# A new written-out order for a two-layer attention and token-MLP kernel: the same operations, other places and other engines

## The chip, the cores and the metric

The kernel runs on one core of a Trainium2 chip. Its time is device microseconds of one execution. Five engines work beside each other, each through its own list of instructions: TensorE (PE in the profile, its weight loads PEld), VectorE (DVE), ScalarE (ACT), GpSimd (POOL) and SyncE (SP), which here only issues DMAs. An instruction that needs the result of another engine waits for a semaphore, and everything behind it on its engine waits too.

## The reference

A stream x of 2048 rows and 512 columns (bf16) passes through four residual steps, A, B, A, B, with the same weights in both rounds. This text calls one round of A and B a layer (layer 1 and layer 2; the code counts 0 and 1).

```
A: h = layernorm(x); q, k, v = h @ wqkv, 32 heads of 16
   p = softmax(q k^T / 4), each row sees itself and the 255 rows before it
   x = x + (p v) @ wo
B: h = layernorm(layernorm(x)); u = gelu(h^T @ w1 + b1), w1: 2048 x 1792, over the rows
   x = x + (u @ w2 + b2)^T, w2: 1792 x 2048
```

## The kernel before, in words

x stays in SBUF as 16 tiles of 128 rows. The rows are taken in four blocks of 512 (the m of `qkv`); in layer 1 the first block is split in two halves of 256. For each tile, `ln_blocks` takes statistics on DVE (L471, L473), the reciprocal deviation as a power on POOL (L484), and the normalised tile xh on DVE (L491). xh is transposed, the first tiles on PE with an eviction by ACT or DVE (L549, L556, L558), all later ones by DMA (L542). Q, K and V are projected by matmuls (L513, which is the line of all matmuls made by the helper `mm_group`).

K is stored "block diagonal" (`kbd`), the two head halves beside each other with zeros between. It gets there straight from PSUM (L582 on ACT, L583 on DVE), or through a staging tile (L594, L596) and then in one of three ways: two masked copies on POOL or DVE (L609) or eight DMAs (L604). V goes into a staging tile (L631 on DVE, L633 on ACT), and four DMAs make the V blocks `vb` (L636).

Attention runs in chunks of 256 or 512 rows. A step of a chunk is a score group on PE (L690, 4 heads at a time), two exponentials on ACT (L705, `pt<-PS`), one to three masks on POOL or DVE (L726), and the weighted sums on PE (L747, operation `pv`). The sums are transposed on DVE (L767), divided (L771, L773 on POOL or DVE) and transposed back (L778). `wo_block` multiplies by wo and adds to x (L789).

B's first product is cut in parts over the rows (`PARTS`): parts whose rows are ready run between the score groups as filler for PE (`u_part`), the last part (L868, `u_last`) runs after the attention, then the gelu on ACT (L883) and the product with w2 (L513, `y_block`), whose result DVE adds to x (L909). In layer 1 these last products run on into the beginning of layer 2's attention; in layer 2 each result tile is stored at once (L955), and the last tile in three pieces (`y_last`, L895, L898).

Weights w1 and w2 come in loads of 128 KB (L803, L815), x, wqkv and wo in loads of 128 to 512 KB (L401, L405, L416). All of SP's loads go through one queue.

The order is written out. The operations are recorded with what they read and write, some of them with alternatives (another engine for the same result: `alts`, for the evictions, masks, products, K copies). `begin_order` decodes `ORDER`, a packed list that names, position by position, the next operation and which alternative it takes; `replay` walks it, hands out buffers in that order and appends each operation to its engine's list; `emit` writes the lists with the waits that the reads, writes and buffer reuse need. No cost or due time is looked at when the kernel is built.

```
        for pos, (idx, alt) in enumerate(order):
            o = self.ops[idx]
            o.eng, o.fn = o.alts[alt][:2]
            self._take(o)
            self.order[o.eng].append(o)
```

Of the kernel before, what the change touches and what calls it, by code (L numbers as in the profile page):

```python
# [11 lines left out]
P = 128  # L12


ORDER = (
    'c-qBQJ&5a87Cw^iym#m24ro9DE$D$>P@zHr1r$&~4;*kn0Tl{p!G#}q!G!|~IH1A-2lN&PwBQ9TIN-tyE*x;-!V50EV3sLdcwrV?xbVUhQ@EI7Sf+5{!o?nq'
    '$20ciz5Hx8yJyB%_g-CH-SeIAd`ALMAW$=FmRTW@UM>_MC=^Pi;EO_mPE}Ps8;@00Q*G-bFh2xcf8YPD^Jy4{4r?wJVNeNZF(i;5j)u<AALc&kTb8BtuoYXD'
    'EV9&YSZ!4!>!g`bN{ewkFV?-!CZqniE{d#Ft%9xV!b#)(TCEaPYV5=_a)q2Md&JD;Y}-<ZEX(4%qNtz|nGh-nqM(nNFd2`>41lrbFj=oV>y08w5=@sO5l;Q9'
    'E5~t`4k7c4g`?**4MwApcs`k)PYEH@>2%p2_m%ug%J;zU^<}w}Bmj_HTwbUu%%gUDrPRKHF)ZpZ8V-j>IkgT#q9zGxwOWL+*Q6H5QAD5FVugcBIS8UCVtAx5'
    'oJ<&u19$iv7cna1#_*YKJ5^OyJ|z~OtkC_q)3F@aao}aY-|XcJja+V-4ePd#=6Nr5$8=54^GwtKgfnf&d1+c%n=zA#x^CzI129br?M|l+Elo!hRD}YZf_Qqu'  # L20
    'SP)3ERD?p|W-T+p<AlWmmz&J>+$%~ixu#_`=S`xiFBAY-2B_6)1cnJql2x_3URO7ptD9B5K6*wd)Vkd{-aVgQFQ<Q>cFUdVVsW`#OsA3K%;)o&*{hi55Q9-J'
    '&$FfBG&||^{?_aDDLp%bAP7veKNy<kcP63}C9PHz{n0aH$ElgsxDhjE)LBq-b-g0Gt{ca(`sEk$b^TQ&DrE65;-xkz7100?E&w~1%|a*V<m_xVrnDCQ9!bX-'
    'm1YXX*h}M)fU!Om&@okIOl(PvC5<{j12J|S3bq}Tigu~!`;_{gMNNZdeg7q;j;bwzsGwS!B?u~0Ziq%Y!^?{V8oI8Zce{fD0`^>Em^H0dLzbj46plFn<Ww=A'
    'FQK`4LOj>DNP1RH&t|jQXq06s1sG+39kbi*t^uyE!Cc~!i-kgzrhK_Xo{tGG>%nMzHqPfML1rY`Bx!fr#C02P^EJAFZ(cjutY58xXXjs)hPF-A3lBL3pX4lJ'
    'o4RQ@9~cBgQ$#}$1OcwgE@B2$AdHBjArra3DN3SFkg5WD1k-axgz>l%2E(u)1b&%$CBINMT;FsZMb~r1oPiq~IYiJfbj!AeLw#WAgbe9`w0dBuuGqvgRI6$j'
    'Lc4<2z`#YeO+!o3Fn0_>IzT9qQcL7U7do+6@7L?yx^*Vrn%pXe80Su@MFqwhm|>=H;=0V37#a(!ArlQI2rlNJAe`WqOfhG#%;{=H-5W~sx^x5=7q*a+gflh$'
    'eZw$Pt#TZr6a%Qw`y4VQmouyne9JOS0EC7qvVzDPj44PKNl{G8B<pp1eIlAyme0J)%S%H$)eL|an)+N(`aLv4B*F~_HO#v|s2W6@$RDsi$nbjkB_tw<aCUYk'
    '2%!wcfUen!F_|78BN06ngymAB$TM;-Nt5|()|t)vvzaWn&qvv;Tm`7MhvtWaKA@`N30<K-=(ly9A_Jd|R8$)In<f)_y+1(=bS0n$TwlMwx<cq7j=u@(C`omM'
    's+WpyhcVx0`At5b6!LM*{CvrmDw0$xmkNc#rysW*%d#2dEs#FcKqmsA;wpwx&^1K`SfV3>fB;P<6ID1nqf~>FlQsVIBw?qUO$1{_QR7&{n2;j^pNrDz@KvRP'
    'TuK<mIr4oZ1y_!9SyUwYJ76btI<*!T3yU5b?QZw{9Hy=d9K2`0HxPs}^t#>t;Lp8&uVtQFrU}$Q`lqt{ZNl~Yf`ICa&~-Y75XsujO{=A87$B%rB7GV}b(9zY'  # L30
    '!{`(WoNg6MMP0AzkT0PA69N(@pXYm16Wzfq^z*(fYqEw}a{7X?cLkw<Ig%y~Rv3X&ok}t$2N6%!f^;N~$NkaC$qf0x1Uyf>-6bt(Dr%$g90?}?KF5_9Bjq&r'
    '9VRfOm7H#+>+RW`V$C>FkB<j`i7}q|K(_<XYPW`Ah;7)b*Etl+sQ&d=xDeCKb@TZ=swXnG*RcqAC>3m#2FEZ|10}nJyGwXDa!fJMLOcUE@4D;t8rCTF_KdDp'
    '|1^yA<<&pVaphmfWICUu<!>~UB*XY_G#-s?$tqjlN}AScVXSKL*K!D9S_VJ=yjH4~LRu`AgEE#cl(BpvpVe)WwLK4sNQCSM`bXp=iwJ^1G+BAkm!89|;E<#0'
    '5m!-^W`k?os-6+90>f~bsiaDi{tQqkm1!RJ6VNdN6KJ;<Xrpm^*cw#FsDIU@*6DORRU@vZyI^4JQ7JM?MU+}7R=i5t^UGK(hjfISwCi<9P;1@T^KGmPwx6?$'
    '*`}Si72oo#we1*=ty>Z<K|oE*NRs|kQo3VFj-qBWDr2RP%}Py=YhYMbK*X6DDpU<N!bV@P(lwST5xh&(i+Q7GS|c{pKw4GeK!HfSMw)Ln+D&j%-rOMigkF)W'
    'tIbAOU&8!+J`XM&6!y_r8jXS!q*_hOK?T1v(t@EBna)rd<f<%4h$aS4NQ;jOl%l*~OW_w9_o&0&&v3hj+gnZ!duhI<*Czn)Jlx^9hb0`)bV%+FN`XV$Zku+n'
    '%>ZN|?LN&sO}kq=zHOhv-X((zp6<=U-J8*Pa_H5QU5DrIHq7vcHy#^*d!K)d4tMK5e>l${9Ua~EIN<K_y7Py7!t>njX^wjX)W6uc-L~877SOvn4xM=XCjR#3'
    'ffxM4i0An?kYc;%9Wwk|$-{APJ07>ksr#_L-FWzK8n-+D0aDygj{&!b@9tr^=Pk!^+<%y7KZ6b2k1gcj|6*(}X#Cwjf54*cklzn(I)3MF&FvFM_fPP5OiFd)'
    'PDWB$dFT6#-?q>0yM*KRNS1zT!}g1NyGbT<D<hdyr!twhb1?I;1+K~*&h7>o9{)0XkL(?vf4BgDKjPoOZ+@F@{L_OaPq}pBkzPEK;jMa+EjG7q-XVq8Cxq-~'
    'fqY-CA5M)9kj(yDwjO2Pn4mw1SmuWW<UnaM{7ypdNwS?t+e|9Z`@ub6^$)5i|0od;xd4x4`DbU#p|J1k!A{$`U5U8saSyKSuRIv-&+SBsdzd5tlMLqG#I842'  # L40
    'njg9Q>mP6%x*dvl<9p-|jZg3K-1a{$!)bv|s~^WdEIxed;iHG!)%)G|$*<zszX32A5e)'
)

def begin_order(n):
# [944 lines left out]
```

## Time and profile before

| | |
|---|---|
| median of 3 runs (lowest to highest) | 437.09 us (436.16 to 437.51) |
| the profiled execution, its own time | 436.27 us |
| its span | 434.5 us |
| granted TensorE clock | 1.0 |
| PE busy | 420.9 us, 97% of the span |
| DVE busy | 322.6 us, 74% |
| ACT busy | 317.0 us, 73% |
| POOL busy | 187.2 us, 43% |
| chain that ended last, by engine | PE 73%, ACT 18%, DVE 6%, DMA 1%, POOL 1% |
| 304 exponentials on ACT | 281.0 us, 1036 ns each |
| 189 masks on POOL, 77 on DVE | 125.9 us, 686 ns each; 29.6 us, 404 ns each |

A line of a group of instructions gives source line, engine, operation, tile written <- tiles read, count, busy us and mean ns. The chain follows the last instruction back to what released it, step by step. A mean over the whole span hides that the stages have different limits, so the table by stretches of time below says more than the shares above.

### The profile page before, as it was taken

Reading aid. Unit: us, or ns where it says so; the run is one execution under the profiler, and the core shown is the slowest. Engines: PE = TensorE matmul, PEld = TensorE weight load, DVE = VectorE, ACT = ScalarE, POOL = GpSimd, SP = SyncE. Lnnn points to the kernel's source line nnn. Section 1 sums busy time; section 2 is a strip of 40 time slices with the busy share of each in tenths; the row PEclk is TensorE's granted clock in tenths of the full one; section 3 lists DMA queues with packets and bytes.
Section 4 is the critical chain, followed back from the end, with each engine's and each line's share of the span. In section 5 each row is a group of like instructions: output and inputs, shape, how many; then the busy total and the mean of one; then the engine's idle time right before and its main releaser. Section 6 shows DMA issues by size and latency. Waiting matters only on the chain.

```text
span 434.5 us, 14318 instructions
## 1 busy us (share of the span) xinstructions
PE 420.9 (97%) x6177; PEld 188.5 (43%) x6177; DVE 322.6 (74%) x629; ACT 317.0 (73%) x364; POOL 187.2 (43%) x277
## 2 busy tenths in 40 slices
PE   7979989999999999999999999999999999999997
PEld 6534333434444444444444444444434444445443
DVE  7998989779996678556777999989788758422205
ACT  5999999999997953606999999899999870520000
POOL 7788865864664620011465554365435221000000
PEclk9999999999999999999999999999999999999999
DMA  8565262302163257723542282240223262747713
GB/s 237 167 125 88 63 127 37 79 5 49 26 166 83 75 152 211 208 62 88 137 110 52 64 147 64 51 77 11 47 64 99 66 175 69 226 140 213 228 32 115
DMA packets 101850, 46.03 MB, mean 106 GB/s; under 512 B 32156, under 2 KB 101788, under 8 KB 101788
## 3 DMA queue, kind: packets, MB, share of 16 engines
q1 hardware_dynamic: 101788, 45.13, 41.7%
q8 instruction: 49, 0.80, 0.8%
q14 instruction: 13, 0.11, 0.1%
HBM read 33.56 MB, written 2.10 MB: 82 GB/s over the span
## 4 chain that ended last, share of the span: by engine, by line
PE 73%; ACT 18%; DVE 6%; DMA 1%; POOL 1%; issue 0%; SPq 0%
PE PS L513 50%; ACT pt L705 17%; PE PS L868 8%; PE PS L690 8%; PE PS L747 7%; DVE stats L471 1%; DMA vb<-vst 1%; DVE xh_sb L491 1%; DVE pt L726 1%; DVE rl L767 1%; DMA x_sb<-in_A_x_dram 1%; POOL pt L726 0%; DVE stg L594 0%; DVE vst L631 0%; SPq L636 0%
## 5 line engine op out<-in xcount | busy, mean ns | idle before, releaser
L705 ACT ACTIVATE pt<-PS 128x1024 bf16<-128x1024 f32 (+1 forms) x304 | 281.0, 1036 | 13.1 <-PE PS L690 11.9
L726 POOL TENSOR_TENSOR pt<-pt,ldm 128x256 int32<-128x256 int32 (+2 forms) x189 | 125.9, 686 | 101.7 <-ACT pt L705 101.1
L513 PE MATMUL PS<-xhT,wqkv 128*128 128x512 bf16 (+1 forms) x288 | 67.8, 357 | 2.7 <-ACT pt L705 1.9
L513 PE MATMUL PS<-xh_sb,w1b 128*128 128x512 bf16 x280 | 69.9, 381 | 0.1
L513 PE MATMUL PS<-uT,w2b 128*128 128x512 bf16 (+2 forms) x308 | 68.3, 360 | 0.0
L690 PE MATMUL PS<-qT,kbd 32*128 32x64 bf16 (+4 forms) x1552 | 60.2, 247 | 3.1 <-ACT pt L705 2.1
L484 POOL TENSOR_TENSOR rstd<-agg,mhalf 128x2 f32<-128x2 f32 (+1 forms) x33 | 23.8, 722 | 66.8 <-DVE agg L473 66.7
L909 DVE SCALAR_TENSOR_TENSOR x_sb<-PS,bcol,x_sb 128x512 bf16<-128x512 f32 x31 | 22.6, 746 | 38.0 <-PE PS L513 37.7
L690 PEld LDWEIGHTS PS<-qT,kbd 32*128 32x128 bf16 x1552 | 22.7, 92 | 61.7 <-ACT pt L705 45.6
L767 DVE STREAM_TRANSPOSE rl<-PS 128x1024 f32<-128x1024 f32 x32 | 39.9, 1248 | 12.3 <-PE PS L747 12.1
L747 PE MATMUL PS<-pt,vb 64*17 64x128 bf16 (+4 forms) x3104 | 43.6, 248 | 2.4 <-DMA vb<-vst 1.1
L471 DVE BATCH_NORM_STATS2 stats<-x_sb 128x6 f32<-128x512 bf16 x64 | 44.2, 693 | 1.5 <-DMA x_sb<-in_A_x_dram 0.8
L883 ACT ACTIVATE uT<-rl,bcol 128x512 bf16<-128x512 f32 x28 | 18.3, 712 | 33.8 <-DVE rl L879 33.8
L513 PEld LDWEIGHTS PS<-uT,w2b 128*128 128x128 bf16 x308 | 27.5, 98 | 31.1 <-issue 3.2
L747 PEld LDWEIGHTS PS<-pt,vb 64*17 64x17 bf16 x3104 | 31.8, 84 | 17.6 <-issue 7.9
L513 PE MATMUL PS<-uT,pt 128*128 128x512 bf16 x168 | 39.2, 379 | 0.0
L868 PE MATMUL PS<-xh_sb,w1b 128*128 128x512 bf16 x168 | 37.7, 379 | 0.0
L513 PEld LDWEIGHTS PS<-xhT,wqkv 128*128 128x128 bf16 x288 | 24.2, 97 | 30.1 <-issue 6.3
L513 PEld LDWEIGHTS PS<-xh_sb,w1b 128*128 128x128 bf16 x280 | 23.7, 98 | 30.8 <-issue 5.9
L513 PE MATMUL PS<-wqkv,xhT 128*128 128x512 bf16 x128 | 34.2, 381 | 0.2 <-DVE stg L594 0.2
L726 DVE TENSOR_TENSOR pt<-pt,ldn 128x256 int32<-128x256 int32 (+1 forms) x77 | 29.6, 404 | 5.3 <-ACT pt L705 5.0
L513 PE MATMUL PS<-wo_sb,oT 128*128 128x512 bf16 x128 | 32.4, 380 | 0.5 <-ACT pt L705 0.5
(62 smaller groups left out, 340.7 us busy)
## 6 DMA issues: line engine op xcount, KB each, us to landing
w1b<-in_B_w_dram SPq DMA_DIRECT2D x112, 128.0 KB, 2.8
w2b<-in_B_w_dram SPq DMA_DIRECT2D x70, 128.0 KB, 2.8
pt<-in_B_w_dram SPq DMA_DIRECT2D x42, 128.0 KB, 3.0
vb<-vst SPq DMA_DIRECT2D x64, 68.0 KB, 2.1
out_dram<-x_sb SPq DMA_DIRECT2D x15, 128.0 KB, 1.8
x_sb<-in_A_x_dram SPq DMA_DIRECT2D x3, 512.0 KB, 6.2
kbd<-stg SPq DMA_DIRECT2D x80, 16.0 KB, 1.9
wqkv<-in_A_wqkv_dram SPq DMA_DIRECT2D x4, 256.0 KB, 5.4
```

The lines of the kernel that those rows point to most:

```text
L471: op("vector:stat", lambda e: e.bn_stats(st[:, 0:6], x_sb[:, t, :]), reads=[f"x{t}"], writes=[("st", i)], cost=dve_cost(512))
L484: op("gpsimd:rstd", lambda e: e.tensor_tensor(rstd[:, t0:t1, 0], agg[:, t0:t1, 1], mhalf[:, 0:1].to_broadcast([P, t1 - t0]), op=ALU.pow), ...
L491: op("vector:xh", lambda e: e.tensor_scalar(xh_sb[:, t, :], x_sb[:, t, :], agg[:, t, 0:1], rstd[:, t, :], op0=ALU.subtract, op1=ALU.mult), ...
L513: return e.matmul(o, lhsT=w, rhs=x, start=start, stop=stop, skip_group_check=True)
L690: last = e.matmul(bank(tt[r // 2], r % 2)[:, base + c0 * 64:base + (c0 + n) * 64], lhsT=kbd[32 * r:32 * r + 32, tk.slot, o, jj].rearrange( ...
L705: op("scalar:exp", lambda e, ts=ts, tp=tp, i=i, cols=cols: e.activation(probs(tp)[:, i, 0:cols, :], pair(ts)[:, :, 0:cols].rearrange("p r ...
L726: return e.tensor_tensor(v, v, m, op=by)
L747: last = e.matmul(bank(t, h)[32 * r:32 * r + 17, i + q0 * 64:i + (q0 + n) * 64], lhsT=vb[64 * h:64 * h + 64, tk.slot, jj, 4 * o + r, :], r ...
L767: op("vector:od", lambda e, t=tod, tr=tr: e.transpose(rl[:, tr.slot:tr.slot + 2].rearrange("p a b -> p (a b)"), pair(t)), reads=[(tod, i) ...
L868: last = e.matmul(bank(tu, tt), lhsT=v()[:, sc - b0, k0 + tt * P:k0 + (tt + 1) * P], rhs=xh_sb[:, sc, :], start=(sc == b0), stop=(sc == NT ...
L883: op("scalar:gelu", lambda e, ft=ft, tt=tt: e.activation(uT[:, ft, :], rl[:, tmps[tt].slot], ACTF.Gelu_apprx_tanh, bias=b1col[:, ft:ft + 1 ...
L909: op("vector:resy", lambda e: e.scalar_tensor_tensor(x_sb[:, t, :], bank(ft), b2col[:, t:t + 1], x_sb[:, t, :], op0=ALU.add, op1=ALU.add), ...
```

## The change

Only `ORDER` is replaced. It still names each of the 2476 operations once; no size, tile, buffer or formula changes. After it, all line numbers are larger by one.

```
--- before.py
+++ after.py
 ORDER = (
-    'c-qBQJ&5a87Cw^iym#m24ro9DE$D$>P@zHr1r$&~4;*kn0Tl{p!G#}q!G!|~IH1A-2lN&PwBQ9TIN-tyE*x;-!V50EV3sLdcwrV?xbVUhQ@EI7Sf+5{!o?nq'
...
+    'c-pmAU5Mk>6+W`>WVP%as)4(pfC37rpcF0WK?Mc0;DEL`pcWO}qJjbrIN*Q^UNA)o3b>$vDGoT`f&&hy#Q_KW;DQT&@WVXJgA0Ce!720Lhb=fTg$?+@4^wcV'
...
 )
```

Decoded, the two lists differ in this:

- Engines, layer 1: masks on POOL 105 to 88, on DVE 25 to 42; products L773 on POOL 12 to 14, on DVE 4 to 2; block-diagonal K copies by DMA 5 to 7, on DVE 2 to 0; the ones of the V staging tile move from POOL to DVE; of two evictions of transposed tiles, the one before the first exponential goes from ACT to DVE, one behind it from DVE to ACT.
- Engines, layer 2: masks on POOL 84 to 87, on DVE 52 to 49; products on POOL 6 to 8, on DVE 10 to 8; K copies by DMA 5 to 2, on DVE 3 to 5, on POOL 4 to 5; evictions of Q on ACT 3 to 6, of V on ACT 4 to 1, straight K pairs on ACT 2 to 1, the rest of each on DVE.
- Loads at the start, by place on SP's list. Before: x tiles 1, 0, 2 to 3, K weights early half, Q early half, x 4 to 7, Q late half, K late half, V weights, b1, b2, x 8 to 11, two of w1, x 12 to 15, the first V-block load, four transposes, wo, one of w1, the second V-block load. After: x tiles 1, 0, 2 to 3, Q early half, K early half, x 4 to 7, K late half, Q late half, V weights, x 8 to 11, b1, two of w1, b2, x 12 to 15, wo, one of w2, one of w1, the first V-block load, four transposes, the second V-block load.
- DVE at the start: the mask constants (L433 and after) now stand behind the statistics of the third and fourth tile.
- PE: the score groups keep their order. Before the second score group stand now one more Q and two more K projections of the first block; the score group that started at 21.31 us and the first weighted sums (21.88 us) change places, so that the score group stands behind the sums; elsewhere single fillers move by one to a few places past a score group, and in the products with w2 at the two ends of a layer the order of the tiles is another.
- The last piece of the result has 128 columns instead of 256.

More of the change, by code (lines that the diff above doesn't have):

```diff
@@ L20 @@
[L20 to L39, printed above, removed]
@@ L42 @@
+    'HJPrmZ2|W-!zsF+ac@h#?chGGXK>fPOWnJ{=!2j-boy1fiyQpx;^0su)?Mog=IPBR@iwTg<LWxR(p-8&-Sx<Zv%4wjZJB;HB-00>b0`|SW@=~Tvvk~#rViq7'
+    'Q@@kiu0Oiz7mmBLk0}lgBw}aIfuSgDWWSJb*T`_|k)x}-r}u`eO-*l#^er^lbU%mFw^Jas10{8H=}nmS0PQG}K8)yVx#ZHf&@{!}7WoGX#~n5~?xr|%+^wSV'
+    'og?J%oM+D1i9L6v4}00;o)f|wdvLqQk2{oW?l~nT-y(1?t{t~OPTVc?xUYqd`=50u^-bD+Lxyiw_FpO2uD=3u=aAjA$gQcvU7NC>f8F8^p6~-8{$GmxU+&c-'
+    '0R'
 )
```

27 lines of the change are left out of this document (22 added, 5 removed).

## The prediction

> **What bounds the kernel now.** I read the profiled execution first by stages (busy time of each engine in six stretches, cut where the chain changes its engine), then the chain that ended last, then the waits of ScalarE, then single loads.
>
> ```profile
> 0.00:9.40 9.40, 7.01 (x72) 5.92 (x72) 6.48 (x26) 4.11 (x8) 7.48 (x16) 1.00 0.78 222
> 9.40:98.00 88.60, 81.62 (x1608) 36.00 (x1610) 78.30 (x157) 87.24 (x101) 66.97 (x98) 1.00 0.43 91
> 98.00:158.60 60.60, 60.07 (x1309) 27.19 (x1310) 48.43 (x92) 55.47 (x59) 34.75 (x48) 1.00 0.35 91
> 158.60:201.00 42.40, 42.40 (x198) 18.82 (x199) 28.14 (x51) 12.26 (x18) 2.07 (x3) 1.00 0.51 137
> 201.00:356.00 155.00, 153.98 (x2627) 64.96 (x2627) 131.27 (x254) 145.87 (x163) 74.48 (x110) 1.00 0.37 85
> 356.00:434.50 78.50, 75.87 (x380) 35.61 (x377) 30.01 (x52) 12.03 (x18) 1.45 (x2) 1.00 0.51 146
> ```
>
> Columns: stretch, length, busy us of PE, PE's weight loads, DVE, ACT, POOL, granted clock, DMA share, GB/s. From the first exponential (9.40) to 98, ACT is busy 87.24 of 88.60 us: that stage lasts as long as ACT's work. From 98 to the end PE is the bound: it idles 0.53, 0.00 and 1.02 us, and the 2.63 us of the last row are the last result and its store. So an order that leaves the work alone can win only in four places: before 9.40, ACT's idle time to 98, about 1.5 us of PE idle later, and the tail.
>
> ```profile
> 21.88 0.86 PE PS L747 x63
> ...
> 22.77 1.25 DVE rl L767
> 24.02 0.76 DVE kbd L583 x2
> ...
> 25.63 0.55 DVE vst L631
> ...
> 28.60 4.01 DMA vb<-vst
> ...
> 32.65 1.52 PE PS L747 x114
> ...
> 34.57 1.03 ACT pt L705
> ```
>
> The waits of ACT between 9.4 and 98 us (total, times, longest):
>
> ```profile
> ACT pt L705 <- PE PS L690: 1.0, 2, 0.7
> ```
>
> The chain (start, us, what) passes the largest hole in ACT's stage: the second load of V blocks (issued 26.64 to 28.60) lands at 32.61 after 4.01 us, where the group's median is 2.1; the weighted sums at L747 wait for it, the next score group stands behind them, and ACT idles 0.68 us before 34.57. Just ahead of it in the queue went 512 KB of wo and 128 KB of w1 (25.47, 26.10).
>
> ```profile
> 5.99 1.80 POOL L461 MEMSET kbd<- 128x2048 f32 x1
> ...
> 6.41 1.43 DVE L433 TENSOR_SCALAR ldm<-tri,half 128x64 int32<-128x64 bf16 x1
> ...
> 10.37 0.33 PEld L513 LDWEIGHTS PS<-xhT,wqkv 128*128 128x128 bf16 x4 [0.21 <-DMA wqkv<-in_A_wqkv_dram]
> ```
>
> ```profile
> vb<-vst SPq DMA_DIRECT2D x64, 68.0 KB, 2.1
> ```
>
> In the order of time PE waits at 10.37 for projection weights, and a small constant on DVE (L433) lasts 1.43 us, until POOL's memset ends at 7.79. The last line gives a load of V blocks, KB and the median us from issue to landing; the landings below are issue times plus such an answer for that load alone.
>
> **The change, part by part.** The program's 2476 operations, sizes and tiles stay. The score groups keep their order, and so nearly do the matmuls: the PE work ahead of most score groups is the same to 0.43 us. Switches of PE between score groups, sums and other matmuls, which cost about 0.1 us each in the trace, come out even (each kind within 3). I cost PE's work at nothing.
>
> *ACT, layer 1:* the same operations, but the eviction of one transposed tile before the first exponential goes to DVE, and another, behind it, comes from DVE: +0.46 us (start to next start of an eviction of 512) in the stage that ACT sets.
>
> *Start:* the early half of K weights swaps its place with Q's. By issue plus landing the fourth and fifth loads landed at 2.19+3.4=5.6 and 2.70+4.4=7.1. The first K projection stood at 7.11 and waited for ACT's eviction (6.97). Now that eviction ends near 6.7 on DVE, but K lands at 7.1: first exponential unchanged, 9.40. L433 moves behind the statistics of tiles 2 and 3, whose rstd waits for POOL's memset anyway: their xh comes about 0.4 us sooner, but PE then stands before a K projection on the late half of K, now the seventh load: 3.80+6.5=10.3. Three projections (0.43 each), a transposed tile (0.24) and a fourth projection with the step to a score group (0.53) put the second score group at 12.4, not 10.97. ACT by then has the two exponentials (2 x 0.905), the added eviction and a Q eviction behind it, so it idles from about 11.7. Summing its operations from 12.8 in the new order gives 22.55 for the exponential that started at 21.62: 0.93 late, of which 0.46 is the eviction.
>
> *Large loads:* x tiles 8 to 11 go right behind the V weights; wo, with a w2 and a w1 load, goes out ahead of the first V-block load, not behind the transposes at 25.47. So nothing large stands before the second V-block load. Its last input on DVE is now late (about 27.1, not 26.17): last issue near 29.15, landing at 2.1 gives 31.3; at 4.0 again, 33.2. The score group ahead of the sums ends near 32, so I take 31.3, the row of an undisturbed queue, as the load ahead is gone. Then ACT runs on: ten starts at 0.905 from 25.3 give 34.3 instead of 34.57, ten more 43.4 instead of 43.98. Ends: 0.6 early if both landings hold; 0.5 late at 34.57 with 4.0 us.
>
> *Masks:* POOL to DVE, 17 in layer 1: DVE 3 x 0.269 + 11 x 0.438 + 3 x 0.516 = +7.2 us, POOL 3 x 0.458 + 11 x 0.743 + 3 x 1.001 = -12.6. Two products go back (DVE -1.5, POOL +2.1), two block-diagonal K copies go from DVE to the DMA queue (DVE -1.4, SP 16 issues x 0.60 = +9.6, off the chain). DVE gains about 4.3 us in a layer in which it idles 10.3 + 12.2 us by the table: hidden. The tight place is 34 to 44 us, where DVE idled 1.6 us and up to 0.9 is added at the transpose of 43.63: hidden too; the cost, if that cover is gone, is 0.9 there.
> Of 77 masks on DVE in the trace four were held while POOL ran (604 to 949 ns; median 415): 1.6 us, so 17 more cost about 0.35.
> [...]
>
> *Layer 2:* ACT loses one K pair (-1.4) and three V evictions (-1.8) and gains three of Q (+1.9); DVE nets -0.7 (masks 4 x 0.269 - 7 x 0.438, products -1.5, Q -2.0; V +2.0, K +2.9); POOL +6.9 with 74.5 of 155 us busy; SP 24 issues fewer. PE covers all (153.98 of 155). Bounds: -1.0, its whole idle time there, to +1.0, the same again; I take 0.
>
> *Tail:* the last piece of the result has 128 columns, not 256: 0.35 for 0.48 on DVE, but a store of 32 KB (2.2 us to landing in the middle of the queue, 64 KB at the end 1.5): -0.1 to +0.6; I take 0.
>
> Sum: +0.46 and +0.47 in the first 13 us; about -1.5 by 44 us, where ACT's restarts after its holes at 24.62, 34.57 and 43.98 cost 0.27, 0.89 and 0.35 by start to start. -0.6 net. The profiled execution took 436.27 (span 434.5 and 1.8 around it), 0.8 under the median of 437.09, against which the result stands: 436.5.
>
> **Rivals.** Under 435.8 or over 438.4 (0.3%) is more than a measurement of this kernel tells from no change.
>
> A, faster: the second score group is not held, because the seventh load lands before 9.6, and ACT's holes at 80.84 and 90.47 (0.32 and 0.52 by start to start) close as well: 0.46 - 2.35 = -1.9, 435.2. For it: no large load stands in the way of V blocks any more. Against it: loads landed in order of issue, and the seventh holds as many bytes as before.
>
> B, slower: the first V-block load is what the early loads now delay. Ahead of it, behind the V weights (landed 4.90+7.6=12.5), stand three loads of 512 KB and four of 128 KB. At the rates seen between landings (1.5 to 2.4 us and 0.4 to 0.6) they drain between 18.6 and 22.1; its own issue, near 16.7 to 18.8, would give 20.9. The new order puts a score group behind the sums that wait for it, so ACT starves when it lands after 22.1, a microsecond for a microsecond. Slow drain and a landing of 4.0 rather than 2.1 together make 24.2: +2.1, with 0.9 - 1.5 from above +1.6, 438.7. Against it: large loads ran at the quick rate from 12.5 to 14.9.
>
> [...]
>
> **How the numbers follow.** Forecast 0.45, C 0.07 (both within 0.3%), A 0.28, B 0.20. Faster 0.28, same 0.52, slower 0.20. The likeliest case alone spans 435.8, where A's side begins, to 437.6 (the late landing, 1.1 over the sum). The range takes in A and, with B, up to 438.6: 434.9 to 438.6.
>
> **What would show it.** Right: first exponential within 0.2 us of 9.40; a hole of ACT before its third or fourth exponential; none near 34.5; 98 to 356 us with the same PE idle time. [...] The forecast is wrong if PE, full until now, idles over 1 us in the second layer or in the last 78 us, where w2 loads have a new order that I cost at nothing: they are covered by PE's 75.87 of 78.5 us, and a late one would cost its delay in full.

## The result, and the profile after

The changed kernel takes **443.04 us** (median of 5 executions, 439.42 to 444.45) against 437.09 before: ratio 1.0133, 95% interval 1.0106 to 1.016. It is slower, by some 6 us, and outside the range of the prediction. Run again among the experiments it took 441.19 (6 executions, 440.09 to 443.45), ratio 1.0113 (1.0085 to 1.014). The middle of all eleven is 442.1.

Two profiled executions of it are read here, because they differ where chance has a part. The first took 443.04 itself (span 441.3), the second had a span of 439.5. By stretches, the first execution (columns as in the table of the prediction):

```profile
0.00:9.40 9.40, 5.80 (x50) 5.06 (x51) 6.63 (x26) 1.97 (x3) 6.89 (x15) 0.97 0.79 230
9.40:98.00 88.60, 78.84 (x1578) 36.41 (x1589) 76.42 (x155) 85.34 (x101) 59.36 (x86) 0.96 0.41 94
98.00:158.60 60.60, 56.90 (x1177) 25.45 (x1182) 50.63 (x99) 55.44 (x60) 31.40 (x45) 1.00 0.30 74
```

and the middle one of these rows in the second:

```profile
9.40:98.00 88.60, 80.62 (x1576) 35.43 (x1573) 76.97 (x157) 84.80 (x98) 59.87 (x88) 0.96 0.43 94
```

ACT, which was busy 87.24 of the 88.60 us from 9.4 to 98, now idles 3.3 and 3.8 us there. PE, full from 98 on before, idles in the first execution's last row, by less than the row looks: 66 of its 6177 matmul records are missing there, and the lags below give 1.5 us. The granted clock from 9.4 to 98 is 0.96; it was 1.00.

To see where the time goes I set the starts of the same score groups beside each other in the traces of before and after. The lag, in us:

| score group (start before) | 8.95 | 19.79 | 21.31 | 27.62 | 34.11 | 99.31 | 130.66 | 200.99 | last matmul |
|---|---|---|---|---|---|---|---|---|---|
| after, first execution | 2.8 | 3.5 | 5.4 | 4.9 | 4.0 | 4.3 | 5.8 | 6.8 | 6.6 |
| after, second execution | 0.1 | 0.7 | 3.5 | 3.9 | 3.3 | 3.3 | 4.2 | 5.3 | 4.8 |

At 200.99 0.9 us of the lag is work that the new order has put ahead of that group, and at 21.31 up to 0.8 us are the weighted sums that have changed places with it. What both executions share are two jumps, one ahead of 21.31 and one ahead of 130.66. In the timeline of PE (start, us, what, in brackets the idle time before and what ended it), the first execution:

```profile
8.53 3.29 PE L514 MATMUL PS<-xhT,wqkv 128*128 128x256 bf16 x16 [2.18 <-DVE ldm L440]
25.68 1.10 PE L748 MATMUL PS<-pt,vb 64*17 64x64 bf16 x64 [2.01 <-DMA vb<-vst]
134.61 1.90 PE L514 MATMUL PS<-xh_sb,w1b 128*128 128x512 bf16 x8 [1.31 <-DMA w1b<-in_B_w_dram]
```

and the second:

```profile
7.19 1.91 PE L514 MATMUL PS<-xhT,wqkv 128*128 128x256 bf16 x16 [0.94 <-DMA wqkv<-in_A_wqkv_dram]
23.59 1.26 PE L748 MATMUL PS<-pt,vb 64*17 64x64 bf16 x64 [2.68 <-DMA vb<-vst]
133.04 1.90 PE L514 MATMUL PS<-xh_sb,w1b 128*128 128x512 bf16 x8 [0.71 <-DMA w1b<-in_B_w_dram]
```

In the first row of the first execution the bracket names a mask constant on DVE, which these matmuls don't read; in both executions they start 0.09 us behind the landing of the early K weights (8.44 and 7.10).

**The first V blocks.** The weighted sums that started at 21.88 wait 2.0 and 2.7 us for the first load of V blocks, which landed at 25.64 and 23.55 (20.38 before). The issues of SP show why it is late, first in the kernel before, then in the second execution:

```profile
8.71 0.40 SPq L444 DMA_DIRECT2D tri<-in_B_b_dram  x1
...
16.27 2.67 SPq L636 DMA_DIRECT2D vb<-vst  x4
```

```profile
5.50 1.98 SPq L402 DMA_DIRECT2D x_sb<-in_A_x_dram  x1
12.00 0.40 SPq L445 DMA_DIRECT2D tri<-in_B_b_dram  x1
...
15.28 0.51 SPq L417 DMA_DIRECT2D wo_sb<-in_A_wo_dram  x1
...
16.90 2.69 SPq L637 DMA_DIRECT2D vb<-vst  x4
```

SP issues nothing from 7.5 to 12.0 (5.4 to 8.7 before). It stands before the load of the bias (L445; 8.71 before, 14.69 in the first execution), which overwrites `tri`, the triangle that the mask constants are made from, and is written to wait for all four blocks of these constants (`reads=LD`). The new order puts one of the operations that make them behind two evictions of K on DVE. DVE in the first execution, the second of the two evictions and the operation:

```profile
14.11 0.41 DVE L595 CAST stg<-PS 128x256 bf16<-128x256 f32 x1
14.43 0.23 DVE L440 TENSOR_SCALAR ldm<-ldm 128x64 int32<-128x64 int32 x1
```

A constant of 0.23 us waits for two evictions, these wait for PE, and behind the bias load on SP stand two loads of 512 KB and four of 128 KB. (That operation reads only the first block, not `tri` any more, so the wait is wider than the data ask for.) The loads go out just ahead of the V blocks and not 5 us before; the last of them lands at 21.45, and the V blocks, issued at 16.9 as they should be, land behind them.

**The clock.** In the second execution the wait costs more than its length of 2.7 us: 4.0, by the estimate in the section on the clock below. By microseconds (columns as above: PE's busy time stands behind the length, the granted clock is third from the end):

```profile
21.00:22.00 1.00, 0.00 (x0) 0.00 (x0) 1.00 (x5) 1.00 (x2) 0.56 (x1) 1.00 1.77 222
...
23.00:24.00 1.00, 0.41 (x32) 0.41 (x40) 0.00 (x0) 0.20 (x1) 0.72 (x2) 0.50 1.01 205
...
30.00:31.00 1.00, 1.00 (x73) 0.73 (x72) 0.89 (x2) 0.54 (x1) 0.83 (x1) 1.00 0.00 0
```

PE stands for 2.7 us; the granted clock is at a half for 6.8 us, from 22.8 to 29.6, the first 0.8 of them still in the stop, and ACT waits for score groups in that time. In the first execution PE stands for 2.0 us at this place, and the granted clock is at a half for 3.4 us, from 25.9 to 29.3.

**The w1 load.** In layer 1's first product PE waits for a w1 load (operation 836) that the kernel before issued as the second of two from 9.98 us on. In the new order it is the seventh of a row of w1 loads that goes out behind K copies and V blocks. SP before, then SP and the chain of after, first execution (start, us, what):

```profile
9.98 0.98 SPq L803 DMA_DIRECT2D w1b<-in_B_w_dram  x2
```

```profile
116.61 5.97 SPq L605 DMA_DIRECT2D kbd<-stg  x8
122.63 2.02 SPq L804 DMA_DIRECT2D w1b<-in_B_w_dram  x2
124.74 2.61 SPq L637 DMA_DIRECT2D vb<-vst  x4
127.40 6.66 SPq L804 DMA_DIRECT2D w1b<-in_B_w_dram  x11
```

```profile
130.62 3.94 DMA w1b<-in_B_w_dram
...
134.61 1.90 PE PS L514 x8
```

**What only the first execution has.** Its fifth load, the early half of K, landed at 8.44 (7.10 in the second execution), and then the first 16 projection matmuls took 3.29 us, not 1.91, at half clock. That is the lag of 2.8 at the first score group.

### The profile page after: what moved, and what is told of

It reads as the page before. It is cut to its first block, busy times and chain, and to the rows that moved or that the text cites. A ratio compares the mean times of both kernels' runs of the same rounds, so it can differ in the third digit from the quotient of the medians.

```text
span 441.3 us, 14245 instructions
## 1 busy us (share of the span) xinstructions
PE 415.0 (94%) x6111; PEld 189.2 (43%) x6177; DVE 325.9 (74%) x642; ACT 315.6 (72%) x362; POOL 183.6 (42%) x268
## 4 chain that ended last, share of the span: by engine, by line
PE 74%; ACT 17%; DMA 3%; DVE 2%; issue 2%; SPq 1%; POOL 0%
PE PS L514 51%; ACT pt L706 17%; PE PS L691 8%; PE PS L869 8%; PE PS L748 7%; DMA w1b<-in_B_w_dram 2%; DMA vb<-vst 1%; SPq L804 1%; DVE stats L472 1%; DMA x_sb<-in_A_x_dram 0%; DVE kbd L584 0%; SPq L637 0%; DVE x_sb L910 0%; DVE agg L474 0%; DVE vst L632 0%
## 5 line engine op out<-in xcount | busy, mean ns | idle before, releaser
L727 POOL TENSOR_TENSOR pt<-pt,ldm 128x256 int32<-128x256 int32 (+2 forms) x175 | 117.0, 688 | 99.2 <-ACT pt L706 98.8
L514 PE MATMUL PS<-xhT,wqkv 128*128 128x512 bf16 (+1 forms) x274 | 66.0, 364 | 6.2 <-ACT pt L706 2.3
L514 PE MATMUL PS<-uT,w2b 128*128 128x512 bf16 (+2 forms) x300 | 69.7, 360 | 0.9 <-issue 0.7
L514 PE MATMUL PS<-xh_sb,w1b 128*128 128x512 bf16 x264 | 66.0, 380 | 4.0 <-issue 1.7
L472 DVE BATCH_NORM_STATS2 stats<-x_sb 128x6 f32<-128x512 bf16 x64 | 43.3, 683 | 2.3 <-DMA x_sb<-in_A_x_dram 1.4
L727 DVE TENSOR_TENSOR pt<-pt,ldn 128x256 int32<-128x256 int32 (+2 forms) x91 | 36.5, 417 | 9.4 <-ACT pt L706 9.0
L514 PE MATMUL PS<-uT,pt 128*128 128x512 bf16 x163 | 41.1, 379 | 0.3
L869 PE MATMUL PS<-xh_sb,w1b 128*128 128x512 bf16 x164 | 38.5, 379 | 0.3
L514 PE MATMUL PS<-wqkv,xhT 128*128 128x512 bf16 x119 | 32.8, 383 | 1.5 <-issue 1.5
L514 PE MATMUL PS<-wo_sb,oT 128*128 128x512 bf16 x118 | 31.5, 380 | 1.9 <-ACT pt L706 1.0
```

Source lines behind the costliest of these rows:

```text
L472: op("vector:stat", lambda e: e.bn_stats(st[:, 0:6], x_sb[:, t, :]), reads=[f"x{t}"], writes=[("st", i)], cost=dve_cost(512))
L514: return e.matmul(o, lhsT=w, rhs=x, start=start, stop=stop, skip_group_check=True)
L727: return e.tensor_tensor(v, v, m, op=by)
L869: last = e.matmul(bank(tu, tt), lhsT=v()[:, sc - b0, k0 + tt * P:k0 + (tt + 1) * P], rhs=xh_sb[:, sc, :], start=(sc == b0), stop=(sc == NT ...
```

## The experiments

Theory 1: the loss is made in SP's queue, by the late constant and by the late w1 load. Theory 2: it lies in the rest of the order (masks moved to DVE, layer 2). Theory 3: the halved clock alone. An edit moves operations in the list before it is replayed; `(a, '<', b)` puts operation a just before b, `'>'` just behind it:

```
-        g.replay(begin_order(len(g.ops)))
+        g.replay(moved(begin_order(len(g.ops)), [(26, '>', 25)]))
```

Operations: 8 and 9 early K and Q weights; 24 to 28 the operations on DVE that make the mask constants, 26 the late one (it makes the second of the four blocks; the expectations, which count operations, call it the third); 29, 30 bias loads; 15 wo; 17 x tiles 12 to 15; 63 first V blocks; 836 the w1 load; 852 w1, 1103 w2. Line numbers of these kernels are larger by up to 48. All times, with the ratio to the kernel before on the same chip:

| kernel | median (executions) | ratio, 95% |
|---|---|---|
| after, again | 441.19 (6) | 1.0113, 1.0085 to 1.014 |
| after, K first | 441.01 (5) | 1.0096, 1.0059 to 1.0132 |
| after, constant early | 439.16 (10) | 1.0045, 1.0021 to 1.007 |
| after, constant early and K first | 438.63 (10) | 1.0035, 1.0018 to 1.0052 |
| after, w1 load early | 440.49 (5) | 1.0087, 1.0053 to 1.0122 |
| **after, constant and w1 load early** | **437.24 (10)** | 1.0006, 0.9987 to 1.0026 |
| the same and K first | 438.26 (12) | 1.0029, 1.0012 to 1.0046 |
| after, bias loads behind | 440.67 (4) | 1.0101, 1.007 to 1.0132 |
| after, V blocks ahead of three loads | 444.45 (4) | 1.0157, 1.0113 to 1.0202 |
| after, PE kept busy | 445.97 (4) | 1.0206, 1.0147 to 1.0266 |
| old order to some 105 us, then new | 437.88 (10) | 1.0016, 0.9993 to 1.004 |
| new with early constant to 109 us, then old | 438.44 (12) | 1.0039, 1.0014 to 1.0063 |
| old, new, old | 439.62 (6) | 1.0066, 1.0041 to 1.0091 |
| before, constant late | 441.45 (4) | 1.0107, 1.008 to 1.0133 |
| before, constant late, wo and w1 first | 439.62 (4) | 1.0069, 1.0044 to 1.0094 |
| before, wo and w1 first | 436.07 (10) | 0.9997, 0.998 to 1.0015 |
| before, wo first | 436.58 (12) | 0.9986, 0.9968 to 1.0005 |
| before, wo first, PE filled at the start | 438.25 (8) | 1.0035, 1.0012 to 1.0057 |

### K first, constant early, and both

Edits: `[(8, '<', 9)]`, `[(26, '>', 25)]`, and both.

> The changed order with one exchange undone: the early half of the K weights goes out fourth again and Q's fifth. Theory 1 (the loss is made in the queue of loads in the first 25 us): K lands near 6 us, PE projects K at about 7.1 and not at 8.53, it is not idle long enough for the clock to be halved, the first exponential is back at 9.4 to 9.6 (12.41 in the changed kernel, 9.40 in the kernel before), but the first load of V blocks still goes out behind the large loads, so that the lag at the score group of 21.31 is 1.5 to 3.5 instead of 5.4: 439.5 to 441 us. [...] Theory 3 (the halved clock alone makes the loss): no halved clock anywhere, lag at 21.31 under 1, near 438.5.

> The changed order with one operation moved: the third block of the mask constant is made on DVE right behind the second and no longer behind two evictions of K. The load of the bias, which waits for it, then goes out near 9 to 10 us and not at 14.69, and with it everything queued behind it on SP. Theory 1: the large loads then go out 3 to 5 us sooner and the first load of V blocks, which waits for late evictions as before, lands between 22.5 and 24 and not at 25.64; K and the halved clock at 8.9 to 12.3 stay, so the first exponential stays at 12.4; the lag at the score group of 21.31 falls from 5.4 to about 3: 440 to 441.5 us. Theory 2: no change in the time, 442.5 to 443.5. Theory 3: the second stretch of halved clock goes with the wait of PE for the V blocks: 441.5 to 442.

> Both moves together: early K weights fourth, Q fifth, and the third mask block made behind the second. Theory 1: first exponential at 9.4 to 9.6, first V blocks landed by 21.5, lag at the score group of 21.31 at most 1, at 44 us 0 or a gain of 0.5; what is left is the wait for a w1 load near 130 (1.5 us) and about 1 us of small pieces behind it: 438 to 439.5 us. Theory 2: above 441. Theory 3: the same as with the exchange of K and Q alone, within 0.5 us.

Measured: 441.01, 439.16, 438.63. The constant alone takes 2.0 us away against the second median of the changed kernel, 3.9 against the first, 3.0 against the middle of the eleven; by the ratios, which allow for the chip, 3.0 and 3.8. That is more than expected. In its profile SP stands no more, V blocks land at 20.48 (issues of SP, then the timeline of ACT):

```profile
8.87 0.40 SPq L455 DMA_DIRECT2D tri<-in_B_b_dram  x1
...
16.20 2.65 SPq L647 DMA_DIRECT2D vb<-vst  x4
```

```profile
19.26 21.23 ACT L716 ACTIVATE pt<-PS 128x1024 bf16<-128x1024 f32 x23
```

23 exponentials without a hole, through the place at 34.57 where the kernel before idled 0.68 us. The lag is 1.0 at 21.31 and -0.8 at 34.11; at 99.31 it is -0.5: up to there the new order is faster than the old one. Then the w1 load takes 1.4 us. So theory 2 falls for the first hundred microseconds. K first was expected to mend the start and did nothing that the intervals can tell, neither alone (441.01 against 441.19) nor with the constant. In its own profile the V blocks wait was still there (2.32 us), and so was the half clock, from 22.4 to 29.2, so that 441.01 is just above the 439.5 to 441 that were expected: the part of theory 1 that blamed the exchange fell.

### Where the rest lies

Edits: the old list up to one score group, then what is left in the order of the new one; the other way round; and in three parts.

> The order of the kernel before up to the score group that starts at 106 us, and behind that the changed order for all that is then left (in it one w1 load, the one that PE waits for at 132.7 in the changed kernel, and three more are already issued in the head). Theory 1: lag 0 up to 106, no wait at 132, and then only the small pieces: 437.3 to 438.5 us. Theory 2: the rest of the order costs as much as half of the loss: above 439.5. Theory 3 (halved clock alone): 437.1, the same as the kernel before within 0.3%.

> The changed order with the mask constant made early, up to the score group of 109 us, and the order of the kernel before behind it. Theory 1: what was left of the loss with the early constant (439.16) lay behind 109 us, in the late w1 load (1.4) and in pieces of the second layer (0.5): 436.4 to 437.3 us. Rival: the w1 loads that the one order has not yet issued crowd the queue at 109 us when the other takes over: above 438.

> The order of the kernel before up to the score group of 17.2 us, then the changed order up to the score group of 109 us, then the order of the kernel before. It keeps of the change what the traces show as a gain (second V blocks no longer behind wo, lag -1.5 between 21 and 38 us with the constant early) and leaves out its start, its late w1 load and its second layer. Theory 1: lag 0 at 17, -0.8 to -1.3 at 38 us, and that to the end: 435.7 to 436.4 us, against 437.0 of the kernel before. Rival: PE, which is full from 98 us on, has other work left in the second part and gives the gain back: 436.8 to 437.3.

Measured: 437.88, 438.44, 439.62. Behind that place the new order costs 0.16% (-0.07 to 0.4) where the w1 load is in time: within what was expected of theory 1. The other two missed. In both, the lag grows by 1.4 us at a new wait behind the seam (in the three parts 0.8 more follows in the second layer); that of the three parts:

```profile
127.03 1.53 PE L795 MATMUL PS<-pt,vb 64*17 64x64 bf16 x128 [1.41 <-DMA vb<-vst]
```

The w1 loads that the one order had not issued yet stand in the queue ahead of V blocks when the other takes over. The three parts also lost 1.6 us at 19.79, because at the first seam projections were left over that now stood ahead of that score group. An order spliced from two good ones is a third order; these two runs say little on the change.

### The w1 load

Edits: `[(26, '>', 25), (836, '<', 866)]`, and `[(836, '<', 866)]` alone.

> The changed order with the mask constant made early, and the one w1 load that PE waits for near 130 us issued nine places sooner in SP's queue, ahead of the K copies of layer 1's end instead of behind them. Theory: the wait of 1.2 to 1.5 us there goes and nothing takes its place, so the median is 437.4 to 438.2 us, against 439.16 with the early constant alone. Rival: the next w1 load of the same product is as late: 438.8 to 439.5.

> The changed order with only the w1 load issued nine places sooner, the mask constant late as it is. Theory 1: the two causes stand apart, one in the first 26 us, one near 130; this takes away the second alone, 1.3 to 1.9 us of the 5.9: 441 to 441.8 us, with no wait of PE near 132. Rival: with all else 4 us late the load is in time anyway by the lateness of PE: no change, 442.7 to 443.5.

Measured: 437.24 and 440.49, that is 1.9 under the kernel with the constant early, and alone 1.6 under the middle of the changed kernel's eleven (0.7 under its second median). On SP the load passes seven other w1 loads and one load of V blocks. The K copies still stand ahead of it, other than the first expectation says, so that no run tells what they do to it. With both operations moved, PE goes through the place without a wait (ten matmuls in a row, 2 and 8 before):

```profile
128.50 2.33 PE L524 MATMUL PS<-xh_sb,w1b 128*128 128x512 bf16 x10
```

and ACT waits 0.4 us in all between 9.4 and 98:

```profile
ACT pt L716 <- PE PS L701: 0.4, 2, 0.2
```

Two of 2476 operations moved, and the changed order takes the time of the kernel before: this is the experiment that settles the cause. With the w1 load alone the wait for V blocks stayed (2.40 us), and most of the loss with it.

### How the late constant acts

Edits on the changed order: `[(15, '>', 63), (1103, '>', 15), (852, '>', 1103)]`, the three loads behind the V blocks; and the six loads ahead of the bias loads, `[(520, '<', 29), (505, '<', 29), (17, '<', 29), (15, '<', 29), (1103, '<', 29), (852, '<', 29), (32, '>', 122), (31, '<', 32)]` (31 and 32 transpose the bias and evict it). On the kernel before: `[(26, '>', 75), (33, '>', 26), (117, '>', 33), (116, '>', 117)]` makes the constant late (75 is the K eviction, the other three read the constant), `[(15, '<', 63), (837, '<', 63)]` puts wo and a w1 load first, and both.

> The changed order, mask constant still late, but the three large loads (wo, 512 KB; one w2 and one w1 load, 128 KB each) moved from just ahead of the first load of V blocks to just behind it. It tells the two halves of theory 1 apart: that SP stands 6 us before the load of the bias, and that large loads are then queued between that and the V blocks. If the large loads are what is met: V blocks go out near 18 and land between 20.5 and 22.5 (25.64 in the changed kernel, 22.3 or less with the constant early), the lag at the score group of 21.31 falls to 1 to 3.5, depending on when K lands in the profiled execution, and the median is 439.5 to 441 us, most of what the early constant gave (439.16). If the stand of SP alone matters, because the x tiles behind it come too late for the V evictions: V blocks land behind 24 and the median stays above 442. Rival (the clock alone): the median goes with the number of stretches at half clock, about 1.5 us each, wherever the V blocks land.

> The changed order with the mask constant left as late as it is, and SP's two bias loads moved behind the six loads that stood behind them (w1, w1, x tiles 12 to 15, wo, w2, w1), still ahead of the first V blocks; PE's transpose of the bias, which no product needs before 150 us, goes behind the first weighted sums so that it does not wait in their place. Theory 1 (the late constant costs only because SP stands before the bias load with that queue behind it): the six loads go out by 10 to 12 us, V blocks land at 20.5 to 22.5, and the median is the one of the early constant, 438.5 to 440. Rival (the constant costs through the masks that read it on POOL and DVE): 442 to 444, as the changed kernel.

> The kernel before, with the two halves of the suspected cause put in: the third mask block (with what reads it) is made behind the two K evictions, as in the changed order, and wo (512 KB) and one w1 load (128 KB) go out ahead of the first load of V blocks. Nothing else of the change is in it. Theory 1: the load of the bias goes out at 12.5 to 13.5 us and not at 8.71, the V blocks land at 23 to 25 and not at 20.38, the sums at 21.88 come 1.5 to 3 us late, a stretch at half clock follows in most executions: 438.5 to 441 us. Theory 2 (the cause lies elsewhere in the order): 436.7 to 437.5, as before.

> The kernel before with only the first half of the suspected cause: the third mask block (with what reads it) is made behind the two K evictions, so that SP stands before the load of the bias; no large load is moved. With both halves put in, the kernel before went to 439.62. If the stand of SP by itself makes the loss (the x tiles 8 to 11 stand behind the bias in SP's queue and come 5 us late, so PE lacks something to project at 14 us): lag of 2 to 2.8 at the score group of 14.1, 438.8 to 439.8 us. If the large loads are needed for it: V blocks land by 21.5, 437.0 to 437.8.

> The kernel before with only the second half: wo (512 KB) and one w1 load (128 KB) go out ahead of the first load of V blocks, the mask constant stays early, so SP does not stand. If large loads ahead of the V blocks delay them by themselves: the last of the V blocks lands after 22, lag 0.5 to 2 at the score group of 21.6, 437.5 to 439. If they only do harm when SP stood before: V blocks by 21.2, and the hole of ACT at 34.57, which wo and the w1 load made by standing ahead of the second load of V blocks, closes: 436.2 to 437.0.

Measured: 444.45, 440.67, 439.62, 441.45, 436.07.

The kernel before with nothing but a late constant loses 4.9 us, more than either expectation allowed; with nothing but the large loads first, it loses nothing. So it is the stand of SP, and what happens to be behind it is only who pays. In the kernel before, that is PE's transpose of the bias, which nobody needs for a long time yet (SP's issues, then PE):

```profile
14.00 0.40 SPq L454 DMA_DIRECT2D tri<-in_B_b_dram  x1
```

```profile
16.12 0.18 PE L459 MATMUL PS<-ident,tri 30*128 30x30 bf16 x1 [2.55 <-DMA tri<-in_B_b_dram]
```

With both halves put in the loss is not larger (439.62), so the large loads are no second half of the cause: that step of my theory fell. The changed order says the same: with the V blocks ahead of the three loads the sums no longer wait for them, but the transposes, now behind those loads, land at 29.78:

```profile
19.89 2.66 SPq L647 DMA_DIRECT2D vb<-vst  x4
...
24.34 6.38 SPq L553 DMA_TRANSPOSE xhT<-xh_sb  x4
```

```profile
29.83 0.60 PE L524 MATMUL PS<-wqkv,xhT 128*128 128x512 bf16 x2 [2.41 <-DMA xhT<-xh_sb]
```

One wait for another. With the bias loads behind the queue and the constant left late, the profile is that of the early constant: bias load at 12.24, V blocks landed at 21.02, lag -0.3 at 34.11 and 0.0 at 99.31, 437.78 in that execution. The masks that read the constant are no cause there. Its median is 440.67, though, from four executions between 437.78 and 442.58, and no trace shows what the longer ones lost. The trace speaks for theory 1, the median leaves it open.

### The clock, and chance at the start

Edits: the matmuls of the score group ahead of the wait (operation 226) five times; the changed kernel again, unedited; and, on the kernel before with `[(15, '<', 63)]`, 13 matmuls of left-over work behind the second transposed tile.

```
+        eng, once, *more = g.ops[226].alts[0]
+        g.ops[226].alts[0] = (eng, lambda e: [once(e) for _ in range(5)][-1], *more)
```

> The changed kernel with the matmuls of one score group (the one at 23.28, the last ahead of the wait for V blocks) issued five times in place of once, to the same place, so that PE works through 1.6 of the 2.0 us in which it waits; the four repeats are work that is left over, nothing else differs. It tells the wait from what the clock adds to it. If the clock is halved because PE stood idle there: no stretch of 0.5 between 25 and 30, the lag still grows by 1.5 to 2 at that place, but 1.2 to 1.6 us of the time are gone: 441.3 to 442 us. If halving has nothing to do with this wait: the stretch stays, 443 to 443.6. If the wait costs nothing by itself and the clock is all: below 440.

> The changed kernel itself, unchanged, for a second profiled execution and for more times beside the kernel before. In its first profiled execution the fifth load (early K) landed at 8.44 and the first four projections ran at half clock (3.29 us for the 16 matmuls, 1.91 in most other profiled executions). Theory 1: these two are chances of an execution and not of the order; what is the order's own is the wait for V blocks (2.0 us) and the wait for the w1 load (1.3 us), which are both there again; median 442 to 444. Rival: the late K is the order's own (K fifth, behind Q): it lands after 8 again, and PE waits for it over 1.5 us.

> The kernel before with wo ahead of the first V blocks, and 13 matmuls of 128x128 on constants (left-over work, written to a bank that nobody reads) behind the second transposed tile, so that PE works from 6.35 to 7.1 and does not stand before the first K projection. In the profiled execution of the kernel with wo alone moved the first 16 projection matmuls took 3.31 us instead of 1.91. If half speed there is what PE's short idle time leads to now and then: 16 matmuls in 1.9 to 2.0 us, no times over 437.5, median 435.5 to 436.3, the fastest of all kernels here. If it has nothing to do with PE's idle time: the same as with wo alone, 436.6, with some times above 437.

Measured: 445.97, 441.19, 438.25. With PE kept busy the wait for V blocks is there (the sums start at 23.44, not 21.88), and no stretch of half clock follows. That prices the two apart, roughly, if one compares what the lag does from the group of 19.79 to that of 34.11 (single executions, in which the V blocks also landed at different times):

| execution | half clock between 20 and 34 us | lag at 19.79, at 34.11 | change |
|---|---|---|---|
| constant early: no wait | none | 0.6, -0.8 | -1.4 |
| PE kept busy | none | 0.8, 0.9 | 0.1 |
| after, first | 3.4 us | 3.5, 4.0 | 0.5 |
| w1 load early | 3.4 us | 1.1, 2.1 | 1.0 |
| after, second | 6.8 us | 0.7, 3.3 | 2.6 |
| K first | 6.8 us | 0.8, 3.0 | 2.2 |

By this estimate the wait by itself costs 1.5 us, one stretch of 3.4 us at half clock 0.4 or 0.9 more, two of them 2.1 or 2.5. But the time got worse, not better, and for another reason:

```profile
23.44 0.83 PE L748 MATMUL PS<-pt,vb 64*17 64x64 bf16 x64 [1.58 <-DMA vb<-vst]
...
37.25 0.26 PE L691 MATMUL PS<-qT,kbd 32*128 32x64 bf16 x7 [1.94 <-issue]
```

PE stands still 1.94 us in the middle of a score group, where it waits for no one. Two more of 1.24 and 1.70 us follow at 145 and 164. So the run doesn't price the clock by its time. The kernel filled at the start shows the same twice (1.15 and 1.29 us at 128.88 and 161.50); until then it had run as hoped (16 matmuls in 1.91 us, lag -0.9 at 34.11), but its times, 437.5 to 439.5, miss what was expected of it. The rival that the clock alone makes the loss does not hold: 1.5 of the 4 us at this place are there without it, and the one execution of the changed kernel with a clock of 1.0 took 439.42.

The changed kernel run again answers what was chance: K landed at 7.10, the 16 matmuls took 1.91, the waits for V blocks and for the w1 load were both there.

### A faster kernel

Edits: `[(15, '<', 63)]` on the kernel before, `[(26, '>', 25), (836, '<', 866), (8, '<', 9)]` on the changed one.

> The kernel before with one operation moved: wo (512 KB) goes out ahead of the first load of V blocks and not behind the transposes. In the run with wo and a w1 load moved the profiled execution gained 0.86 us at the score group of 34.1 and kept 0.4. If it is wo that stood ahead of the second V blocks, the hole of ACT there closes (second V blocks landed by 31.5, not 32.61): 435.9 to 436.6, against 436.6 to 437.1 of the kernel before. Rival: the w1 load that stays there, or four stores of V blocks in any queue, make the 4.0 us: no gain.

> The changed order with all three moves: mask constant early, w1 load early, early half of K ahead of Q's. Theory 1: the exchange of K and Q costs less than 0.5 us once the constant is early, because both are needed before the first score group: 436.6 to 437.4, the same as with the two moves (437.24) and as the kernel before. Rival: the fifth load is now and then 1.5 us late (8.4 instead of 7.0) and K there is worse than Q: 0.5 to 1 faster than with two moves, 436.2 to 436.7.

Measured: 436.58 and 438.26. wo ahead of the V blocks is worth 0.14% (-0.05 to 0.32) and 0.03% with the w1 load: no kernel here beats the one before by more than can be told from no change, though the hole at 34.57 is closed in all of them. K first is not better than Q first here either (438.26 against 437.24, where the intervals meet), and it misses the 437.4 that were expected at most; its profiled execution, 440.15, has two stretches of half clock, from 7.9 and from 25.0 us.

## Why the prediction was wrong

**The step that failed: the queue ahead of the first V blocks.** The prediction says that what it drew nearer was the second V-block load and takes the first as landing where it did; late, it is rival B, 0.20. The chain of conditions in B came true: the early loads drained at 21.45 in the second execution (18.6 to 22.1 was given), the V blocks landed at 23.55 (24.2 at worst), ACT then waited 2.24 us for the score group behind the sums. What was not seen is why B had to come true: SP stands before the bias load until the last mask constant is made. The prediction, and the list of the change ahead of it, moved the mask constants "behind the statistics of tiles 2 and 3", but left out that one of them had gone on behind two evictions of K, that the bias load waits for it, and that six loads stand behind the bias load on SP. Against B it set that the queue ran quickly from 12.5 to 14.9; with SP standing the queue ran low then. In the second execution the DMA share falls from 1.06 (10 to 12 us) to 0.41 (12 to 14). Of the 5.6 us between the forecast and the middle of the eleven, the late constant makes 3.0.

**The size of B.** It was priced at a microsecond for a microsecond, 2.1, and 438.7. The halved clock behind such a wait stood nowhere in the working; by the table above it makes the 1.5 us of the wait into 1.9 to 4.0. So the term was too small, and the range, which ended at 438.6, with it.

**The w1 load.** The new order of the w2 loads was put at nothing, with a warning for the last 78 us, where no load came late; of the w1 loads only one at the start was followed. The one late load came at 130, in the other product, and cost 0.7 to 2.2 us of waiting, 1.9 by the runs. Both lists of loads have two of w1 near the start, but they are other ones: operation 836 is one of them before and not after. SP's 16 more issues of K copies, 9.6 us "off the chain", stand ahead of it in the queue too; no run moved them.

**What held, and what was half as large.** The first exponential, 9.40, held, by the second execution (timeline of ACT; the 128x512 pair is the second group):

```profile
9.48 1.94 ACT L706 ACTIVATE pt<-PS 128x1024 bf16<-128x1024 f32 x2
...
12.25 1.08 ACT L706 ACTIVATE pt<-PS 128x512 bf16<-128x512 f32 x2
...
25.44 1.94 ACT L706 ACTIVATE pt<-PS 128x1024 bf16<-128x1024 f32 x2 [2.24 <-PE PS L691]
```

In the first execution, where K came at 8.44, it was 3 us late, beyond any bound given. The second score group was held as forecast, but to 11.90 and not to 12.4 (10.97 before):

```profile
11.90 0.29 PE L691 MATMUL PS<-qT,kbd 32*128 32x128 bf16 x8
```

The late half of K, which it waits behind, landed at 9.78, not 10.3. So the 0.93 at the exponential of 21.62 came out as 0.5 (second execution) and 0.4 (constant early). With the constant early the hole at 34.57 closed as forecast, and the exponential of 43.98 starts 0.6 early: the net of -0.6 is what was forecast, made of +0.4 and -1.0 in place of +0.93 and -1.5. That both terms were half a microsecond too large is luck. Masks on DVE are hidden. No run shows the loss by longer masks on DVE that C (0.07) stands for; what the runs show in its place is a lag that is flat from 37 to 127 us in both executions, and a mask on DVE that lasts 417 ns on average, 404 before. Of the 20 between 34 and 98 us two take over 600 ns (679 and 736):

```profile
L727 DVE TENSOR_TENSOR pt<-pt,ldn 128x256 int32<-128x256 int32 (+2 forms) x91 | 36.5, 417 | 9.4 <-ACT pt L706 9.0
```

Layer 2 and the tail, 0 within 1.0 and -0.1 to 0.6, are not nothing: in the kernel with both operations moved the lag is 0.1 at 130.66 and 1.1 at the last matmul, and the rest of the span is 0.2 longer, at the upper end of the bounds. Nearly all of it comes at one place, ahead of the score group of 288.36, where PE waits for an exponential:

```profile
288.11 1.40 PE L758 MATMUL PS<-pt,vb 64*17 64x64 bf16 x96 [1.00 <-ACT pt L716]
```

Ten of the eleven other profiled executions that follow the new order there lose 0.2 to 1.0 at this group (one of seven with the old order, 0.55); why, no run shows. That is as much as the early stage gains. The forecast of 436.5 is close to the time that the order takes (437.24) without the two operations that it did not follow, but the gain in it is not shown (ratio 1.0006).

## What to carry to other kernels

When a small operation moves, look up not only who reads it but which DMA waits for it and what stands behind that DMA on its queue: a constant of 0.23 us held six loads for 3 to 6 us, and moving the victims within the queue only changed who waited. A stop of the matrix engine of 2 to 3 us in a full stretch should be priced with the half-clock stretch that may follow it, which here put 0.4 to 2.5 us on top of 1.5. And a load that had been issued 120 us ahead of its use is worth a line of its own in the working when it moves to the end of the queue.

## What the runs showed of the hardware that was not expected

**Half clock in single executions.** Of 98 executions of the kernel before, 76 had a mean granted clock of 1.0 (0.998 and above) and a median of 436.5 us, 21 had 0.995 to 0.997 and 437.9: by this estimate a stretch of 3.4 us at half clock costs about 1.4 us there. All but one of the eleven executions of the changed kernel were at 0.996 to 0.988.

**When the clock was halved.** The trace keeps the granted clock with its times. In the 18 profiled executions that have such a record, all 11 halved stretches begin a whole number of 3.41 us behind its first entry: in the first execution of the changed kernel at 8.86 and 25.93, one time and six times 3.41 behind 5.45, each 3.41 long; in the second at 22.76, five times 3.41 behind 5.69, 6.8 long. With the traces cut into windows of this length from the first entry on, all nine windows at full clock in which PE was idle for more than 1.7 us were followed by half clock, two of the six with 1.4 to 1.7, and none with less. In the first execution the windows ahead of the two halved stretches held 2.50 and 2.32 us of idle time; in the kernel before no window held more than 1.24, and none was followed by half clock. Where the half clock went on for a second 3.41 us (second execution, K first), PE had been idle for 0.8 or 0.9 us in the first. The stop of 1.58 us with PE kept busy, which was followed by none, fell into two windows; that its place decided this is my reading, as no run moved a stop alone.

**Half speed ahead of the clock's record.** With wo first, the first 16 projections took 3.31 us, after an idle time of 0.77, in a stretch whose clock reads 1.00 (PE's timeline, then the stretches):

```profile
7.29 3.31 PE L523 MATMUL PS<-xhT,wqkv 128*128 128x256 bf16 x16 [0.77 <-ACT xhT L568]
```

```profile
8.00:10.00 2.00, 2.00 (x11) 1.41 (x10) 1.93 (x9) 1.21 (x3) 0.70 (x1) 1.00 1.13 342
```

The idle time is not what made them slow: the four transposes ahead of it already took 307 ns each, 222 in the kernel before. In this trace the record of the clock begins at 10.19 us, with full clock, and the 1.00 ahead of that stands for no entry. The first matmuls of the kernel start some 107 ns apart in every profiled execution, and the record begins between 4.5 and 7.0 us in 15 of the 18, at 10.2 here and with the constant early and K first (16 projections in 3.40), and at 13.75 with the V blocks moved (3.57). Of the first four transposes, at 5.08, the starts are 0.06 us apart in the kernel before, whose record begins ahead of them at 5.01, and 0.10 in the first execution of the changed kernel, whose record begins behind them at 5.45. By these times full speed came with the first entry of the record, and late in the three; filling PE until 7.4 in one execution, whose record begins at 7.0, can't tell whether that helps. A mean clock of 1.0 does not rule it out.

**One load's landing varies.** The fifth load landed between 6.9 and 8.5 us in the profiled executions, whichever tile it carried; both K and Q are needed before the first scores, which fits that their exchange was worth nothing that could be told.

**Stops of PE in the kernels with matmuls added.** The two kernels with left-over matmuls (32 and 13 more) have five stops of 1.15 to 1.94 us that no wait explains; in the other profiles none is longer than 0.62. The two of the filled kernel:

```profile
128.88 0.24 PE L700 MATMUL PS<-qT,kbd 32*128 32x128 bf16 x4 [1.15 <-issue]
...
161.50 0.59 PE L523 MATMUL PS<-xh_sb,w1b 128*128 128x512 bf16 x2 [1.29 <-issue]
```

The page of after has a DMA queue that it calls "instruction", 49 packets of 16 KB:

```profile
q8 instruction: 49, 0.80, 0.8%
```

By the starts of these packets in the trace, each of the five stops begins 0.7 to 1.2 us after one of them has started. The kernel before has 49 such packets too and no such stop. What the packets have to do with the stops, and why PE stands there, no run shows.
